# A head's rounding cast moves from the Vector engine to Pool, in a bucketed attention with a gated convolution

## The chip, the cores and the metric

The kernel runs on one core of a Trainium2 chip. The core has a matrix engine (PE, with its weight loads shown apart as PEld), a vector engine (DVE), a scalar engine (ACT), Pool (GpSimd), and SP, which here only issues DMAs. Each engine works through its own queue in order, and the engines wait for each other by semaphores. The metric is the device time of one execution in microseconds (us). "The profile" is one execution seen by the hardware profiler, "the trace" its single instructions.

## The reference

Four batches, eight heads, 768 positions, head size 64. Queries and keys are hashed into six bits, a query sees only the keys of its own bucket, and the result of the attention goes through a causal convolution of five taps, a sigmoid gate and two matrices of 512 by 512.

```python
q_bits = (np.einsum('bhsd,dk->bhsk', q, proj) > 0).astype(np.int64)
k_bits = (np.einsum('bhsd,dk->bhsk', k, proj) > 0).astype(np.int64)
mask = q_bucket[:, :, :, None] == k_bucket[:, :, None, :]
scores = scale * np.matmul(q, k.transpose(0, 1, 3, 2))
scores = np.where(mask, scores, -1000000000.0)
attn = np.exp(scores - np.max(scores, axis=-1, keepdims=True))
attn = attn / (np.sum(attn, axis=-1, keepdims=True) + 1e-09)
attn_out = np.matmul(attn, v)
# x is attn_out with the heads side by side, xp is x with 4 rows of zeros ahead
for k in range(K):
    gate_pre += conv_w[k][None, None, :] * xp[:, k:k + S, :]
gate = 1.0 / (1.0 + np.exp(-gate_pre))
val = x @ w_val
return (gate * val @ w_out).astype(np.float32)
```

## The kernel before

**Units and tiles.** A unit is one head of one batch, 32 in all. A unit has six tiles of 128 queries, so there are 192 tiles, and the main loop makes one step (k) for each. A step works on several tiles at once, each at another stage: the row maxima of tile k (`nm`, L238, DVE), a factor and a shift for each row (`gs` L244, `nb` L248, DVE), the scores of tile k+1 (`s`, L232, PE), the exponentials of tile k (`p`, L256, ACT, with the row sums by the accumulator), the row sums and reciprocals of tiles k-2 and k-1 (L262 and `ri` L266, DVE, on even steps), the normalisation of tile k-2 (L271, Pool, in place), the transposes of tile k-3 (`tp`, L280, PE), and their copies to SBUF (`pt`, L289, ACT). The product with the values (`av`, L303, PE) follows in pieces.

**Exactness by two parts.** The scores are made by matmuls in the rounded type fp32r. A head's queries and keys, which lie in one tile `r` of 128 rows (64 of queries, 64 of keys), are split into a rounded part and a remainder. `prep(i)` does it for unit i: it takes four tiles (`aq`, `ak`, `bq`, `bk`, from a pool `stk` with two of each), writes the rounded copy of `r` into `aq` (L166), the remainder `r - aq` into `bq` (L168, Pool), and six DMAs on SP then put the halves where the two score matmuls want them: `ak<-aq` and `bk<-aq` (L169, L170), `bk<-bq` (L171), `bq<-aq` (L172), and the bits of the hash, `aq<-u` and `ak<-u` (L174, L175). The last line also asks for the tile `r` of a unit five further on (L147). The first unit has its own way (`first_prep`).

**When it runs.** `prep(i+1)` is a generator. It is started in the last step of unit i-1, so a whole unit of six tiles lies between its start and the first scores that need it, and each step takes one piece of it: the cast in one step, the subtraction with the DMAs in the next. With it run other generators: the weights (`load_weights`, `split_weight`, `from_float64`: in the shape that the timed kernel is given they come as 64-bit floats and are unpacked by L90 on ACT, L92, L93, L96, L99, L100 and L108 on DVE, L110 and L112 on Pool; two tiles `w` take turns), the convolution (L332, L334 on DVE, one tap for each step), and the second half (`moe`: L365, L390 on PE, L370, L374 on DVE, `hl` L376 on Pool; `xh` L323 and `xl` L324 split its input). The weights are unpacked beside the first nine units; from then on the second half of a batch runs beside the next batch.

**What sets the order.** On PE, DVE, ACT and Pool the order of the instructions is the order of the code (`manual_schedule`). The order of SP's DMAs is left to the framework, which places them by its own estimate of when each can go. So a change in the code of one engine can reorder SP's queue.

Of the kernel before, what the change touches and what calls it, by code (L numbers as in the profile page):

```python
# [26 lines left out]
def kernel(  # L27
# [10 lines left out]
    nc = tc.nc  # L38
# [104 lines left out]
    def load_raw(i):  # L143
        if i < len(units):
            b, h = units[i]
            raws[i] = raw.tile([P, S], FP32, name="r")
            nc.sync.dma_start(out=raws[i], in_=qk[b, h])  # L147

    def load_values(i):
        b, h = units[i]  # L150
        if h % 2 == 0:
            vts[i] = vp.tile([P, KB, P], FP32, name="vt")
            nc.sync.dma_start(out=vts[i], in_=v[b, h // 2])
        else:
            vts[i] = vts[i - 1]

    def prep(i):

        if i >= len(units):
            return  # L160
        b, h = units[i]
        j = h % 4
        load_values(i)
        r = raws[i]
        aq, ak, bq, bk = stacks[i] = [stk.tile([P, S], FP32R, name=nm) for nm in ("aq", "ak", "bq", "bk")]
        nc.vector.tensor_copy(out=aq, in_=r)  # L166
        yield
        nc.gpsimd.tensor_tensor(out=bq, in0=r, in1=aq.bitcast(FP32), op=ALU.subtract)  # L168
        nc.sync.dma_start(out=ak[0:D].bitcast(FP32), in_=aq[D:P].bitcast(FP32))  # L169
        nc.sync.dma_start(out=bk[0:D].bitcast(FP32), in_=aq[D:P].bitcast(FP32))  # L170
        nc.sync.dma_start(out=bk[D:P].bitcast(FP32), in_=bq[D:P].bitcast(FP32))  # L171
        nc.sync.dma_start(out=bq[D:P].bitcast(FP32), in_=aq[0:D].bitcast(FP32))  # L172
        u = cur["u"]
        nc.sync.dma_start(out=aq[D:M].bitcast(FP32), in_=u[32 * j:32 * j + 2 * NB].bitcast(FP32))  # L174
        nc.sync.dma_start(out=ak[D:M].bitcast(FP32), in_=u[32 * j + 2 * NB:32 * j + 4 * NB].bitcast(FP32))  # L175
        load_raw(i + 5)
        if j == 3 and i + 1 < len(units):
            yield
            yield from bits(i + 1)
# [6 lines left out]
    def bits(i):  # L186

        u = stk.tile([P, S], FP32R, name="u", bufs=2)
        for hf in range(2):
            yield  # L190
            sl = slice(hf * HS, (hf + 1) * HS)
            z = side_tile()
            for jj in range(4):
                nc.tensor.matmul(out=z[32 * jj:32 * jj + 32, 0:HS], lhsT=proj_sb,
                                 rhs=raws[i + jj][:, sl], start=True, stop=True,
                                 tile_position=(0, 32 * jj))
            nc.vector.tensor_scalar(out=u[:, sl], in0=z[:, 0:HS], scalar1=rows_sb[:, 0:1], scalar2=rows_sb[:, 1:2],
                                    op0=ALU.is_ge, op1=ALU.mult)
        cur["u"] = u
# [242 lines left out]
    with tc.manual_schedule(engines=ENGINES):  # L442
# [3 lines left out]
        first_prep()  # L446
        weights = [[load_conv(), load_weights(0)], [load_weights(1)]]
        preps = [first_bits(), prep(1)]
        scores(0)
        step(weights[0])  # L450
        step(weights[1])
        turn = 0
        for k in range(N + LAG + 1):
# [15 lines left out]
            if k + 1 < N:  # L469
                if tiles[k + 1][0] != tiles[k][0]:  # L470
                    finish(preps)
                    preps = [prep(tiles[k + 1][0] + 1)]
                scores(k + 1)
# [83 lines left out]
```

## Time and profile before

| | |
|---|---|
| median of 3 runs | 639.09 us (638.87 to 639.24) |
| the profiled execution | 637.56 us |
| its span, first to last instruction | 635.6 us |
| mean granted clock of PE | 0.989 |
| cast L166, 31 times on DVE | 20.6 us |
| subtraction L168, 31 times on Pool | 58.4 us |
| normalisation L271, 192 times on Pool | 220.0 us |

A row of the timeline reads: start, duration, engine, line, operation, output and inputs, shape, how often, and in brackets the idle time of the engine ahead of it with what ended that. SPq is the queue in which SP issues its DMAs. In the table by stretch each engine's busy time stands with its number of instructions, then the granted clock of PE, the share of the DMA engines and their rate. A row of the chain of waits is a start, a length and what the end waited for in that time. A line like L166 is a line of the program printed above.

### The profile page before, as it was taken

Reading aid. Unit: us, or ns where it says so; the run is one execution under the profiler, and the core shown is the slowest. Engines: PE = TensorE matmul, PEld = TensorE weight load, DVE = VectorE, ACT = ScalarE, POOL = GpSimd, SP = SyncE. Lnnn points to the kernel's source line nnn. Section 1 sums busy time; section 2 is a strip of 40 time slices with the busy share of each in tenths; the row PEclk is TensorE's granted clock in tenths of the full one; section 3 lists DMA queues with packets and bytes.
Section 4 is the critical chain, followed back from the end, with each engine's and each line's share of the span. In section 5 each row is a group of like instructions: output and inputs, shape, how many; then the busy total and the mean of one; then the engine's idle time right before and its main releaser. Section 6 shows DMA issues by size and latency. Waiting matters only on the chain.

```text
span 635.6 us, 10630 instructions
## 1 busy us (share of the span) xinstructions
PE 590.1 (93%) x3496; PEld 424.3 (67%) x3496; DVE 465.9 (73%) x1064; ACT 421.7 (66%) x881; POOL 364.7 (57%) x326
## 2 busy tenths in 40 slices
PE   4689888878999999999999999999999999999997
PEld 2465554555567777676667877677667777776895
DVE  5789897999986766668675877578685787665532
ACT  3487776767778666667787766677778677675400
POOL 1375868577765764567653776466562677544221
PEclk9899998998999999999999999999999999999999
DMA  6533535443332334343433333343422223300111
GB/s 243 128 101 86 139 96 138 112 134 81 104 80 58 83 75 123 82 105 96 104 80 79 88 80 110 80 121 80 120 57 61 57 53 79 86 18 2 50 51 50
DMA packets 23269, 56.76 MB, mean 89 GB/s; under 512 B 4296, under 2 KB 4296, under 8 KB 23216
## 3 DMA queue, kind: packets, MB, share of 16 engines
q1 hardware_dynamic: 23072, 56.06, 32.9%
q8 instruction: 28, 0.46, 0.3%
q14 instruction: 25, 0.20, 0.1%
q10 hardware_dynamic: 144, 0.03, 0.0%
HBM read 23.12 MB, written 6.29 MB: 46 GB/s over the span
## 4 chain that ended last, share of the span: by engine, by line
PE 64%; DVE 18%; ACT 10%; issue 3%; DMA 3%; POOL 0%; DVEq 0%; ACTq 0%
PE av L303 16%; PE s L232 15%; PE tp L280 12%; PE m L390 8%; PE m L365 7%; DVE nm L238 6%; ACT p L256 4%; DVE g L334 3%; ACT pt L289 3%; ACT x L311 2%; DMA w<-in_w_out_dram 2%; DVE aq L166 1%; PE tp L365 1%; PE tp L390 1%; PE s L390 1%
## 5 line engine op out<-in xcount | busy, mean ns | idle before, releaser
L271 POOL TENSOR_SCALAR p<-p,ri 128x768 f32<-128x768 f32 x192 | 220.0, 1150 | 200.3 <-DVE nb L248 157.6
L256 ACT ACTIVATE p<-s,nb,gs 128x768 f32<-128x768 f32 x192 | 192.7, 1004 | 49.7 <-DVE nb L248 44.6
L289 ACT COPY pt<-tp 128x384 f32<-128x384 f32 x384 | 166.2, 485 | 86.0 <-PE tp L280 85.0
L238 DVE TENSOR_REDUCE nm<-s 128x1 f32<-128x768 f32 x192 | 182.4, 950 | 52.8 <-PE s L232 52.6
L280 PEld LDWEIGHTS tp<-ident,p 128*128 128x128 f32 x1152 | 130.4, 142 | 74.2 <-issue 47.3
L280 PE MATMUL tp<-ident,p 128*128 128x128 f32 x1152 | 165.4, 280 | 4.5 <-ACT pt L289 1.6
L232 PE MATMUL s<-ak,aq 76*128 76x384 f32 x384 | 118.6, 390 | 32.2 <-ACT p L256 25.4
L303 PE MATMUL av<-pt,vt 128*64 128x384 f32 x768 | 146.9, 504 | 0.0
L232 PE MATMUL s<-bk,bq 128*128 128x384 f32 x384 | 101.6, 346 | 0.0
L232 PEld LDWEIGHTS s<-ak,aq 76*128 76x128 f32 x384 | 59.4, 195 | 48.9 <-ACT p L256 39.3
L303 PEld LDWEIGHTS av<-pt,vt 128*64 128x64 f32 x768 | 47.4, 137 | 63.3 <-issue 62.7
L334 DVE SCALAR_TENSOR_TENSOR g<-x,cw_sb,g 128x768 f32<-128x768 f32 x64 | 78.4, 1225 | 0.2
L232 PEld LDWEIGHTS s<-bk,bq 128*128 128x128 f32 x384 | 71.9, 194 | 0.5 <-issue 0.5
L376 POOL TENSOR_TENSOR hl<-ht,hh 128x384 fp32r<-128x384 f32 x32 | 33.4, 1044 | 45.5 <-DVE hh L374 45.5
L168 POOL TENSOR_TENSOR bq<-r,aq 128x768 fp32r<-128x768 f32 x31 | 58.4, 1885 | 0.5 <-DVE aq L166 0.5
L311 ACT COPY x<-av 64x384 f32<-64x384 f32 x64 | 30.4, 475 | 33.5 <-PE av L303 32.9
L365 PE MATMUL m<-xh,wv 128*128 128x384 f32 x200 | 42.7, 337 | 0.0
L248 DVE TENSOR_SCALAR nb<-nm,gs 128x1 f32<-128x1 f32 x192 | 40.1, 209 | 3.5
L370 DVE TENSOR_TENSOR ht<-m,g 128x384 f32<-128x384 f32 x25 | 13.9, 555 | 35.4 <-PE m L365 32.0
L256 ACT ACTIVATION_READ_ACCUMULATOR p<-s,nb,gs 128x1 f32 x192 | 39.1, 204 | 0.0
L324 POOL TENSOR_TENSOR xl<-x,xh 128x384 fp32r<-128x384 f32 x32 | 33.5, 1066 | 9.5 <-DVE xh L323 9.5
L390 PE MATMUL m<-wo,hh 128*128 128x512 f32 x144 | 38.1, 394 | 0.0
(84 smaller groups left out, 475.6 us busy)
## 6 DMA issues: line engine op xcount, KB each, us to landing
r<-in_qk_dram SPq DMA_DIRECT2D x32, 384.0 KB
vt<-in_v_dram SPq DMA_DIRECT2D x16, 384.0 KB
out_dram<-o SPq DMA_DIRECT2D x24, 256.0 KB
ak<-aq SPq DMA_DIRECT2D x31, 192.0 KB
bk<-aq SPq DMA_DIRECT2D x31, 192.0 KB
bk<-bq SPq DMA_DIRECT2D x31, 192.0 KB
bq<-aq SPq DMA_DIRECT2D x31, 192.0 KB
w<-in_w_val_dram SPq DMA_DIRECT2D x4, 512.0 KB
```

Of the source, the lines that this page charges most:

```text
L168: nc.gpsimd.tensor_tensor(out=bq, in0=r, in1=aq.bitcast(FP32), op=ALU.subtract)
L232: nc.tensor.matmul(out=s[:, hf, 0:HS], lhsT=lq[0:n, qs], rhs=rk[0:n, hf * HS:(hf + 1) * HS], start=n == M, stop=n == P)
L238: nc.vector.tensor_reduce(out=nm, in_=s[:, :, 0:HS], axis=AX.XY, op=ALU.max, negate=True)
L256: nc.scalar.activation(out=p, in_=s[:, :, 0:HS], func=AF.Exp, bias=nb, scale=gs.pop(k), accum_out=sm[:, k % 2, 0:1])
L271: nc.gpsimd.tensor_scalar(out=p, in0=p, scalar1=rcs.pop(k), scalar2=1.0, op0=ALU.mult, op1=ALU.mult)
L280: nc.tensor.transpose(out=tp[:, n * P:(n + 1) * P], in_=p[:, kb * P:(kb + 1) * P], identity=ident)
L289: nc.scalar.copy(out=pt[:, :, qo:qo + P], in_=tp[:, 0:HS].rearrange("p (a b) -> p a b", b=P))
L303: nc.tensor.matmul(out=av[s * D:(s + 1) * D, 0:HS], lhsT=vt[:, kb, hh * D:(hh + 1) * D], rhs=pt[kb // 3][:, kb % 3, :], start=(kb == 0), s ...
L311: nc.scalar.copy(out=x[hh * D:(hh + 1) * D, o:o + HS], in_=av[s * D:(s + 1) * D, 0:HS])
L334: nc.vector.scalar_tensor_tensor(out=g, in0=x[:, k:k + S], scalar=w, in1=g, op0=ALU.mult, op1=ALU.add)
L365: nc.tensor.matmul(out=acc[:, 0:HS], lhsT=wv[wi][:, c, j * P:(j + 1) * P], rhs=xs_[(c, o)][xi], start=(m == 0), stop=(m == 11))
L390: nc.tensor.matmul(out=acc, lhsT=hs[(o, j)][hi][:, tb * P:(tb + 1) * P], rhs=wo[wi][:, j, :], start=(m == 0), stop=(m == 11))
```

## The change

One line: the rounded copy of a head's `r` into `aq` is made by Pool instead of DVE. The subtraction that follows, the DMAs, the tiles and the place in the generator stay as they were.

```diff
         aq, ak, bq, bk = stacks[i] = [stk.tile([P, S], FP32R, name=nm) for nm in ("aq", "ak", "bq", "bk")]
-        nc.vector.tensor_copy(out=aq, in_=r)
+        nc.gpsimd.tensor_copy(out=aq, in_=r)
         yield
         nc.gpsimd.tensor_tensor(out=bq, in0=r, in1=aq.bitcast(FP32), op=ALU.subtract)
```

What that moves, at three places. First Pool, in a unit whose step also has weights to split (`w_848` is a weight tile, `p` the tile that is normalised); a plus marks a row that only the changed kernel has here:

```order
 L271 TENSOR_SCALAR p<-p,ri 128x768 x4
 L110 TENSOR_TENSOR w_848<-w_848,wv_118 128x512
+L166 CAST aq<-r 128x768
 L271 TENSOR_SCALAR p<-p,ri 128x768
 L168 TENSOR_TENSOR bq<-r,aq 128x768
```

The cast stands one normalisation ahead of the subtraction, as it belongs to the step before it, and it follows the weights' subtraction directly.

Then DVE at the same place in the program (`s_1182` is the pair of row sums, `nm` the row maxima of the next tile):

```order
 L334 SCALAR_TENSOR_TENSOR g<-x,cw_sb,g 128x768
 L96 SCALAR_TENSOR_TENSOR w_950<-w_950,o 128x512
-L166 CAST aq<-r 128x768
 L238 TENSOR_REDUCE nm<-s 128x1
 L262 TENSOR_SCALAR s_1182<-sm 128x2
```

The cast is gone between the last weight operation of one step and the row maxima of the next.

Last SP's queue, the DMAs behind that unit's subtraction (`r` is the load of a unit five further on, `vt` the values, `w_1273` a weight tile):

```order
 L170 DMA bk<-aq 64x768
 L171 DMA bk<-bq 64x768
-L147 DMA r<-in_qk_dram 128x768
-L153 DMA vt<-in_v_dram 128x768
-L172 DMA bq<-aq 64x768
-L174 DMA aq<-u 12x768
+L174 DMA aq<-u 12x768
+L153 DMA vt<-in_v_dram 128x768
+L172 DMA bq<-aq 64x768
+L147 DMA r<-in_qk_dram 128x768
 L136 DMA w_1273<-in_w_out_dram 128x1024
 L175 DMA ak<-u 12x768
```

The load of `r` went from directly behind `bk<-bq` to directly ahead of the weights, and the bits `aq<-u` went to the front. The same is found at the next such load (`w_1712`), and at the one before (`w_848`) only the bits moved forward.

## The prediction

> **What bounds the kernel now.** I read the page's busy times first, then the chain of work that ended last with its shares by line, then busy time by stretch.
>
> ```profile
> span 635.6 us, 10630 instructions
> PE 590.1 (93%) x3496; PEld 424.3 (67%) x3496; DVE 465.9 (73%) x1064; ACT 421.7 (66%) x881; POOL 364.7 (57%) x326
> core 0: us, PE busy (x) PEld busy (x) DVE busy (x) ACT busy (x) POOL busy (x), PEclk, DMA share, GB/s
> 80.00:100.00 20.00, 16.79 (x94) 10.81 (x96) 19.62 (x41) 14.59 (x33) 13.47 (x12) 0.94 0.38 90
> 520.00:560.00 40.00, 40.00 (x239) 30.30 (x240) 26.91 (x65) 28.77 (x63) 22.29 (x20) 1.00 0.29 74
> by line: PE av L303 16.5%; PE s L232 15.4%; PE tp L280 11.7%; PE m L390 7.9%; PE m L365 6.6%; DVE nm L238 6.0%; ACT p L256 4.3%; DVE g L334 3.1%; issue 3.1%; ACT pt L289 2.7%; ACT x L311 2.0%; DMA w<-in_w_out_dram 1.7%; DVE aq L166 1.4%; PE
> ```
>
> PE is the bound of the whole, 590.1 of 635.6 us, but not of every stage. From 520 to 560 us it is busy all 40.00 us, and DVE with 26.91 has room. From 80 to 100 us it is DVE that is full (19.62 of 20.00) and PE waits 3.2 us. So DVE time is worth something up to about 165 us, where the weights are unpacked beside the heads, and next to nothing after it. The cast that moves stands in the chain with 1.4% of 635.6 us, that is 8.9 us: the ceiling of the gain. The group and its places in the chain (start, us):
>
> ```profile
> L166 DVE CAST aq<-r 128x768 fp32r<-128x768 f32 x31 | 20.6, 665 | 0.2
> 20.54 1.05 DVE aq L166
> 60.73 0.46 DVE aq L166
> 76.30 1.39 DVE aq L166
> 94.17 0.47 DVE aq L166
> 111.99 0.55 DVE aq L166
> 130.18 0.47 DVE aq L166
> 146.75 1.39 DVE aq L166
> 163.95 0.47 DVE aq L166
> 320.62 0.47 DVE aq L166
> ```
>
> 31 casts cost 20.6 us of DVE; a third of them is in the chain at all. The other twenty are hidden by PE; taking them away gives nothing.
>
> **What the cast costs on Pool.** No row of before shows a one-input cast on Pool. The nearest is Pool's own normalisation, also one input and the same tile size:
>
> ```profile
> 109.67 0.91 POOL L271 TENSOR_SCALAR p<-p,ri 128x768 f32<-128x768 f32 x1
> ```
>
> The other end is the two-input subtraction L168 with 1.82 us (its row stands below). I see no reason for less than 0.9. I take 0.91, the row it is nearest to, where DVE leaves it alone, and keep 1.82 for the range.
>
> [...]
>
> In the late stage the cast falls into Pool's idle time ahead of the next normalisation. The tightest place, Pool and then PE's transposes of the last tile:
>
> ```profile
> 436.29 1.67 POOL L271 TENSOR_SCALAR p<-p,ri 128x768 f32<-128x768 f32 x1 [0.48 <-ACT pt L289]
> 439.75 1.62 POOL L271 TENSOR_SCALAR p<-p,ri 128x768 f32<-128x768 f32 x1
> 442.28 0.85 PE L280 MATMUL tp<-ident,p 128*128 128x128 f32 x6 [0.16 <-ACT pt L289]
> ```
>
> Pool idles 0.48 us where the cast of 0.91 goes, so what stands behind it comes 0.43 us later; the normalisation that ends at 441.37 is used at 442.28, 0.91 us of slack. Nothing is lost; with 1.82 us it would be 1.34 late and cost PE 0.43 here.
>
> **Where the removal pays.** The place at 76.30, DVE, Pool, ACT and PE:
>
> ```profile
> 76.07 1.20 POOL L112 TENSOR_TENSOR wv<-w 128x512 fp32r<-128x512 f32 x1
> 76.30 1.39 DVE L166 CAST aq<-r 128x768 fp32r<-128x768 f32 x1
> 78.92 0.68 DVE L96 SCALAR_TENSOR_TENSOR w<-w,o 128x512 int32<-128x512 int32 x1
> 79.10 0.99 ACT L256 ACTIVATE p<-s,nb,gs 128x768 f32<-128x768 f32 x1 [0.95 <-DVE nb L248]
> 80.35 1.82 POOL L168 TENSOR_TENSOR bq<-r,aq 128x768 fp32r<-128x768 f32 x1
> 80.83 1.76 DVE L332 TENSOR_SCALAR g<-x,cw_sb 128x768 f32<-128x768 f32 x1
> ```
>
> The rows show a hold: DVE's cast started 0.23 us after Pool's L112 and ended 0.42 after it (77.69 against 77.27), and L332 ended 0.42 after L168 (82.59 against 82.17). A DVE copy, or a DVE operation with two inputs in SBUF, that starts second waits for Pool's instruction to end. The new cast is one more such instruction: 77.27 to 78.18. Without L166 the chain on DVE would reach L96 at 77.53, 1.39 earlier; it is held to 78.18. L96 then runs to about 78.75, Pool's normalisation takes 0.91 behind it, so L168 starts near 79.63 and not at 80.35, and L332 ends 0.72 earlier. **Gain 0.72**, not 1.39.
>
> At 94.17 the same hold turns against the change:
>
> ```profile
> 91.46 1.29 POOL L110 TENSOR_TENSOR w<-w,wv 128x512 f32<-128x512 f32 x1
> 92.01 1.56 DVE L334 SCALAR_TENSOR_TENSOR g<-x,cw_sb,g 128x768 f32<-128x768 f32 x1
> 93.49 0.68 DVE L96 SCALAR_TENSOR_TENSOR w<-w,o 128x512 int32<-128x512 int32 x1
> ```
>
> Pool's cast is ready when L110 ends at 92.75, waits for L334 to 93.57 and runs to 94.4; L96, held behind it, ends near 95.03. Now DVE is through with L96 and its own cast at 94.64 (94.17 and 0.47 in the chain), and the reduction nm follows: it will start 0.39 later than now. **A loss of 0.39**, and the same at 130.18.
>
> At 146.75 the wait of PE is long, so the full 1.39 comes back; PE is then in the chain on its own for some 9 us:
>
> ```profile
> 150.69 0.61 PE L232 MATMUL s<-ak,aq 76*128 76x384 f32 x2 [2.08 <-ACT p L256]
> 153.00:156.00 3.00, 3.00 (x14) 2.29 (x11) 2.96 (x8) 2.14 (x5) 2.48 (x4) 0.56 0.71 205
> 156.00:159.00 3.00, 3.00 (x20) 1.73 (x18) 2.68 (x5) 2.59 (x6) 0.77 (x1) 1.00 0.32 70
> 159.00:162.00 3.00, 2.76 (x20) 2.33 (x19) 2.35 (x9) 2.25 (x6) 2.10 (x3) 1.00 0.05 8
> ```
>
> Behind the idle 2.08 us PE's granted clock is 0.56 for 3 us: 1.3 us of work lost. With 0.7 us of idle time I expect this stretch to go; DVE, which is next with idle 0.04, 0.32 and 0.65 us in these rows, lets some **0.8** through.
>
> [...]
>
> The rest: 44.25 gives 0.23 (ACT waits no longer than that), 60.73 gives 0.46, 111.99 gives 0.55, 163.95 gives 0.47, 320.62 and its like near 466 us give 0.2 each, since the cast holds L334 for part. At 20.54 there is nothing to gain:
>
> ```profile
> 46.19 0.99 ACT L256 ACTIVATE p<-s,nb,gs 128x768 f32<-128x768 f32 x1 [0.23 <-DVE nb L248]
> 28.06 0.98 PE L232 MATMUL s<-ak,aq 76*128 76x384 f32 x2 [2.31 <-issue]
> ```
>
> PE stands 2.31 us until the second head's copies have landed. The subtraction, now behind cast and normalisation, ends some 0.4 later, and with it the last copy (bq<-aq, L172); the first half of the scores does not need that one. I charge **0.2**.
>
> **What moves on SP's queue.** In the unpacking stage the load of a later head (r) goes from ahead of the value tile to just ahead of the weight load:
>
> ```profile
> 101.99 0.48 SPq L172 DMA_DIRECT2D bq<-aq  x1
> 103.52 6.17 DMA w<-in_w_out_dram
> r<-in_qk_dram SPq DMA_DIRECT2D x32, 384.0 KB
> w<-in_w_out_dram SPq DMA_DIRECT2D x4, 512.0 KB
> 109.72 0.71 ACT L90 ACTIVATE o<-w 128x512 f32<-128x512 f32 x1 [0.82 <-DMA w<-in_w_out_dram]
> ```
>
> ACT already waits 0.82 us for this weight tile, and its 6.17 us from issue to landing are in the chain. r will now go out behind L172, just ahead of it, and travel in its time. Bound: nothing, or the whole travel of r, by the weights' own rate 6.17 x 384 / 512 = 4.6 us. I take **1.0**, nearer to nothing, since the bytes that go out up to the weights are the same as before and only their start is later. The next such load (w_1712) I leave at 0 for the same reason.
>
> **Sum.** 0.23 + 0.46 + 0.72 - 0.39 + 0.55 - 0.39 + 1.39 + 0.47 + 0.4 = 3.44; clock 0.8; minus 0.2 and 1.0: **3.0 us less**. The profiled execution took 637.56 us, 1.96 over its span; the median of the runs is 639.09, 1.5 above it, and I take the difference off the median: **636.1 us**.
>
> **Rivals.**
> - *DVE's L96 gets in ahead of Pool's cast* at 94.17 and 130.18. Then both give 0.47: 1.7 us more, **634.4**. For it: DVE's instructions follow each other without a gap. Against: Pool has been waiting since 92.75. 15%.
> - *The slow clock stays* at 153 us, or comes at another place: **636.9**. 10%.
> - *A slow cast*, 1.82 us: at 20.54, 76.30, 94.17 and 130.18 another 0.91 each, 3.6 in all: **639.7**, no change. 13%.
> - *The weights come late* (slower). At both loads that now have r directly ahead, the weights wait for all of r, 4.6 us each instead of 1.0 and 0; ACT holds its queue for each. The change without any lateness is worth 3.44 + 0.8 - 0.2 = 4.0, so it decides from 4.0 us of lateness in all: 639.1 - 4.0 + 9.2 = **644.3**, and half of it already gives 639.7. For it: L90 waits now, and the load is in the chain. Against: the bytes ahead of the weights are the same. 10%.
> - *The cast doesn't move the chain*: Pool reaches it so late that the copies to ak and bk, on SP behind it, hold the next head. It would show as PE waiting for DMAs at a head's first tile; the copies have five tiles of time, so 4%, near **639**.
>
> **How the numbers follow.** The forecast has the remaining 48%. The range takes the first rival with a full return of the weights' 1.0 at the lower end, and, at the upper, the slow cast and rather more than half of the late weights: 632.8 to 640.5. About 0.2% (1.3 us) is what a measurement can tell from no change. Faster by more than it: most of the forecast, the first rival and most of the second, 0.63; within it, 0.22; slower, 0.15.
>
> **What would show it.** Right: a Pool cast near 0.9 us alone and up to 1.6 behind a DVE operation; DVE busy by some 20 us less, PE idle by some 3 us less and only up to 165 us; L96 at 94 us ended later than L334 by a Pool cast; L90 waiting about 1.5 us for the weights. Wrong: a cast over 1.3 us alone, transposes that wait for Pool after 200 us, or a span that changes after 200 us by more than 1 us.

## The result, and the profile after

| | before | changed |
|---|---|---|
| median | 638.98 us (637.55 to 639.24, 4 runs) | 632.86 us (632.47 to 634.94, 4 runs) |
| the profiled execution | 637.56 us | 634.94 us |
| its span | 635.6 us | 633.2 us |

The ratio is 0.991, with a 95% interval of 0.9883 to 0.9937. The forecast was 636.1 us, 3.0 less than before; measured here are 6.1 less, and 4.6 less in a second series further below. The profiled execution of the changed kernel is the longest of its four, so its trace shows less of the gain than the median does. That has to be explained too.

From the page of the changed kernel: the busy times, the shares of the chain by engine, and two groups of instructions (the number behind the bar is the busy time, the next one the mean in ns).

```profile
PE 591.4 (93%) x3496; PEld 426.2 (67%) x3496; DVE 451.3 (71%) x1033; ACT 421.1 (67%) x881; POOL 386.0 (61%) x357
PE 69%; ACT 14%; DVE 12%; issue 2%; DMA 2%; POOL 0%; SPq 0%; ACTq 0%; POOLq 0%; DVEq 0%
L166 POOL CAST aq<-r 128x768 fp32r<-128x768 f32 x31 | 27.8, 897 | 0.0
L96 DVE SCALAR_TENSOR_TENSOR w<-w,o 128x512 int32<-128x512 int32 x8 | 8.0, 1002 | 0.0
```

DVE lost the 20.6 us of its casts, yet its busy time fell by 14.6 only. Of the 6.0 us between, about 3.5 went into other DVE instructions that now take longer (L96 1.9 us, L262 2.4, L92 and L93 0.7 each, and some take a little less); the other 2.5 us are overlap, since the records of the casts reached into those beside them and busy time counts such a stretch once. The row of L96 in the kernel before shows it at 760 ns:

```profile
L96 DVE SCALAR_TENSOR_TENSOR w<-w,o 128x512 int32<-128x512 int32 x8 | 6.1, 760 | 0.0
```

Where the gain is, the table by stretch tells: first the stage with weights and then the one without, of before and then of the changed kernel.

```profile
0.00:165.00 165.00, 133.45 (x768) 87.17 (x769) 142.22 (x312) 111.22 (x237) 102.77 (x93) 0.96 0.44 122
200.00:600.00 400.00, 392.37 (x2370) 286.98 (x2370) 283.22 (x663) 282.10 (x588) 232.33 (x207) 1.00 0.31 80
```

```profile
0.00:165.00 165.00, 136.25 (x777) 90.16 (x778) 138.99 (x308) 113.00 (x241) 114.02 (x105) 0.95 0.44 122
200.00:600.00 400.00, 393.14 (x2372) 288.12 (x2373) 276.17 (x646) 279.43 (x586) 240.49 (x225) 1.00 0.31 79
```

In the first 165 us PE is busy 2.8 us longer and gets through 777 matmul instructions where it was 768. From 200 to 600 us PE is busy 393.1 of 400 us and was 392.4: nothing to win there, with the cast gone from DVE or not.

Two places of the changed kernel in rows of the timeline. At 92 us, the hold that the prediction charged:

```profile
91.61 1.55 DVE L334 SCALAR_TENSOR_TENSOR g<-x,cw_sb,g 128x768 f32<-128x768 f32 x1
92.29 1.55 POOL L166 CAST aq<-r 128x768 fp32r<-128x768 f32 x1
93.08 1.31 DVE L96 SCALAR_TENSOR_TENSOR w<-w,o 128x512 int32<-128x512 int32 x1
96.92 1.01 PE L232 MATMUL s<-ak,aq 76*128 76x384 f32 x2 [2.33 <-ACT p L256]
```

Pool's cast is issued at 92.29 and stands behind L334, which ends at 93.16; it ends at 93.84, 0.68 us later. L96, issued at 93.08, ends only 0.55 us behind that: 1.31 us, where it took 0.68 at this place before. At 148 us, where the prediction expected most:

```profile
147.86 0.82 POOL L166 CAST aq<-r 128x768 fp32r<-128x768 f32 x1
148.25 0.98 DVE L96 SCALAR_TENSOR_TENSOR w<-w,o 128x512 int32<-128x512 int32 x1
149.56 0.62 PE L232 MATMUL s<-ak,aq 76*128 76x384 f32 x2 [0.41 <-ACT p L256]
153.00:156.00 3.00, 2.44 (x15) 1.64 (x15) 2.97 (x8) 2.59 (x6) 2.40 (x3) 1.00 0.89 232
```

PE waits 0.41 us where it waited 2.08, and the granted clock behind it is 1.00 where it was 0.56.

### The profile page after: what moved, and what is told of

Its sections match the earlier page's. It is cut to its first block, busy times and chain, and to the rows that moved or that the text cites. A ratio compares the mean times of both kernels' runs of the same rounds, so it can differ in the third digit from the quotient of the medians.

```text
span 633.2 us, 10639 instructions
## 1 busy us (share of the span) xinstructions
PE 591.4 (93%) x3496; PEld 426.2 (67%) x3496; DVE 451.3 (71%) x1033; ACT 421.1 (67%) x881; POOL 386.0 (61%) x357
## 4 chain that ended last, share of the span: by engine, by line
PE 69%; ACT 14%; DVE 12%; issue 2%; DMA 2%; POOL 0%; SPq 0%; ACTq 0%; POOLq 0%; DVEq 0%
PE av L303 19%; PE s L232 17%; PE tp L280 12%; PE m L390 8%; PE m L365 7%; ACT p L256 6%; ACT pt L289 4%; DVE nm L238 3%; ACT x L311 3%; PE tp L365 1%; PE tp L390 1%; PE s L390 1%; DVE u L197 1%; PE tp L194 1%; DVE g L334 1%
## 5 line engine op out<-in xcount | busy, mean ns | idle before, releaser
L271 POOL TENSOR_SCALAR p<-p,ri 128x768 f32<-128x768 f32 x192 | 215.9, 1129 | 173.8 <-DVE nb L248 149.6
L238 DVE TENSOR_REDUCE nm<-s 128x1 f32<-128x768 f32 x192 | 182.5, 951 | 64.3 <-PE s L232 64.2
L303 PE MATMUL av<-pt,vt 128*64 128x384 f32 x768 | 147.6, 506 | 0.0
L303 PEld LDWEIGHTS av<-pt,vt 128*64 128x64 f32 x768 | 47.6, 137 | 63.7 <-issue 63.1
L334 DVE SCALAR_TENSOR_TENSOR g<-x,cw_sb,g 128x768 f32<-128x768 f32 x64 | 77.9, 1217 | 0.2
```

Of the source, the lines that this page charges most:

```text
L238: nc.vector.tensor_reduce(out=nm, in_=s[:, :, 0:HS], axis=AX.XY, op=ALU.max, negate=True)
L271: nc.gpsimd.tensor_scalar(out=p, in0=p, scalar1=rcs.pop(k), scalar2=1.0, op0=ALU.mult, op1=ALU.mult)
L303: nc.tensor.matmul(out=av[s * D:(s + 1) * D, 0:HS], lhsT=vt[:, kb, hh * D:(hh + 1) * D], rhs=pt[kb // 3][:, kb % 3, :], start=(kb == 0), s ...
L334: nc.vector.scalar_tensor_tensor(out=g, in0=x[:, k:k + S], scalar=w, in1=g, op0=ALU.mult, op1=ALU.add)
```

## The experiments

All kernels but the first, which is the changed kernel again, differ from it in the engine of this one cast, for some units (and one makes a second cast); `i` is the unit. "Pool 1 to 10" below is the kernel with the cast on Pool for units 1 to 10 (the stage with weights) and on DVE behind them.

| cast on | median us (range, runs) | before, same series | ratio, 95% interval |
|---|---|---|---|
| Pool, all (the change again) | 633.59 (632.70 to 635.84, 6) | 638.17 | 0.9928, 0.9912 to 0.9944 |
| Pool 1 to 10, DVE behind | 632.98 (632.43 to 633.83, 4) | 638.17 | 0.9917, 0.9903 to 0.9931 |
| DVE 1 to 10, Pool behind | 638.15 (637.16 to 639.29, 11) | 638.17 | 0.9999, 0.9990 to 1.0009 |
| ACT 1 to 10, Pool behind | 631.20 (630.26 to 632.04, 4) | 638.17 | 0.9888, 0.9873 to 0.9902 |
| Pool 5 and 9 only | 636.10 (635.37 to 637.51, 8) | 638.07 | 0.9974, 0.9962 to 0.9985 |
| Pool 1 to 10 without 5 and 9 | 636.45 (634.95 to 638.75, 12) | 638.07 | 0.9973, 0.9958 to 0.9987 |
| DVE, and a second one on Pool | 642.69 (642.01 to 644.39, 6) | 638.07 | 1.0078, 1.0064 to 1.0093 |
| Pool 2 to 10 | 633.84 (633.17 to 634.96, 6) | 638.07 | 0.9934, 0.9921 to 0.9947 |
| Pool 1 to 10, but 6 and 8 on ACT | 632.06 (631.60 to 632.13, 4) | 638.38 | 0.9897, 0.9880 to 0.9913 |
| Pool 1 to 10, but 6 and 8 on DVE | 633.21 (632.54 to 633.51, 4) | 638.38 | 0.9916, 0.9901 to 0.9931 |
| ACT 2 to 10, DVE else | 631.23 (630.75 to 632.34, 4) | 638.38 | 0.9889, 0.9873 to 0.9905 |
| ACT, all | 632.06 (630.80 to 632.81, 6) | 637.77 | 0.9904, 0.9885 to 0.9923 |

The kernels do not all have the same order of DMAs on SP. The weight loads that are issued near 103 and 139 us and unpacked near 109 and 144 us have `r` directly ahead of them in the changed kernel, the change again, Pool 1 to 10, Pool 2 to 10 and Pool 1 to 10 without 5 and 9; in the others, those with ACT and those with 6 and 8 on ACT or DVE among them, the DMA directly ahead is the one of before. No kernel changes that order alone; what can be said of it stands with the prediction's terms below.

To read a trace place by place, I compare the start of the row maxima (L238) of each of the 192 tiles with the same tile in the trace before, and take by how much this lead or lag changes from the last tile of one head to the second of the next. That is what a place costs (+) or returns (-), in us, whatever came ahead of it. The first column is the time of the place in the trace before.

```
place        Pool again  Pool 1-10  Pool 2-10  dup    ACT 1-10  6, 8 on ACT  6, 8 on DVE
44.7         -0.48       -0.47      -0.47     +0.63   -0.47     -0.47        -0.48
61.1         -0.48       -0.49      -0.49     +0.65   -0.44     -0.47        -0.45
77.6         -1.06       -1.07      -0.39     +0.72   -1.21     -1.05        -1.01
94.6         +0.16       +0.16      +0.15     +0.62   -0.48     -0.48        -0.01
130.6        +0.16       +0.16      +0.17     +0.64   -0.47     -0.46         0.00
148.1        -1.22       -1.05      -1.03     -0.68   -1.31     -0.99        -1.82
```

("dup" is the kernel with a second cast on Pool. Where a slow stretch that starts between 131 and 139 us stands ahead of the place at 148.1, as in dup and in the kernel with 6 and 8 on DVE, part of its loss seems to be made good there.)

### The change once more, and its two halves

**The change again**, to see what of 3.0 against 6.1 us is chance:

> The changed kernel once more, with several runs of both kernels on one chip. The two profiled executions differ by 2.6 us, the medians by 6.1. Theory A (the gain is the casts on DVE's chain, some 2.5 to 4 us, and the rest is in which stretches of the first 160 us PE's clock is granted at half): the runs of each kernel spread over about 2 to 3 us, the difference of the medians lies between 3 and 6 us, and an execution with no half-clock stretch has the shorter span. Rival B (the profile hides a gain that is there in every run): the difference stays at 6 us with both spreads under 1 us.

Measured: 633.59 us, 4.6 below the before of its series; with the first four, ten executions of the changed kernel lie between 632.47 and 635.84. The gain is real in each of them, and how large it is varies by 3 us.

**Pool in the stage with weights only:**

```diff
-        nc.gpsimd.tensor_copy(out=aq, in_=r)
+        (nc.gpsimd if i <= 10 else nc.vector).tensor_copy(out=aq, in_=r)
```

> The cast runs on Pool for units 1 to 10 only, from unit 11 on DVE as before. Theory A: all of the gain lies in the stage in which the weights are unpacked; the time is that of the changed kernel within 0.6 us (0.2 us each may be lost at two places near 319 and 465 us). Rival C (Pool and DVE trade time in the late stage too, and PE gains there): at least a third of the gain, 2 us, is lost.

**Pool behind it only:**

```diff
-        nc.gpsimd.tensor_copy(out=aq, in_=r)
+        (nc.gpsimd if i > 10 else nc.vector).tensor_copy(out=aq, in_=r)
```

> The cast runs on DVE for units 1 to 10 as before, from unit 11 on Pool. Theory A: the time of the kernel before, at most 0.6 us less. Rival C: 2 us or more below the kernel before.

Measured: 632.98 and 638.15 us. The first half is the whole change (5.2 us, not distinguishable from 4.6); the second half is worth nothing to within 0.1%. At the two places late in the run for which the prediction wrote 0.2 us each, the row maxima come 0.12 us earlier in the trace, and two tiles later that is gone.

**ACT in place of Pool in the stage with weights:**

```diff
-        nc.gpsimd.tensor_copy(out=aq, in_=r)
+        if i <= 10:
+            nc.scalar.copy(out=aq, in_=r)
+        else:
+            nc.gpsimd.tensor_copy(out=aq, in_=r)
```

> The cast runs on ACT for units 1 to 10 and on Pool from unit 11. It is DVE's relief without Pool's new instruction in the early stage. Theory A with the hold (a Pool cast holds DVE's L96 at 94 and 130 us by some 0.6 us, at 76 and 147 by 0.3): about 1.5 to 2 us under the changed kernel, less what ACT's own cast of some 0.8 us delays of the exponentials. Rival D (the hold costs nothing, since DVE's chain waits for PE anyway): not below the changed kernel, and above it by the ACT time, up to 0.8 us for each of ten units.

Measured: 631.20 us, better than both kernels. The same place as above in its trace (the added lines shift the numbers by three: L235 is the score matmul):

```profile
91.44 0.83 ACT L167 CAST aq<-r 128x768 fp32r<-128x768 f32 x1
91.75 0.68 DVE L96 SCALAR_TENSOR_TENSOR w<-w,o 128x512 int32<-128x512 int32 x1
94.96 0.62 PE L235 MATMUL s<-ak,aq 76*128 76x384 f32 x2 [1.33 <-ACT p L259]
```

ACT needs 0.83 us for the cast, Pool alone 0.82, but L96 takes 0.68 us beside it and not 1.31, and PE waits 1.33 and not 2.33 us.

### Two places alone, and the others

```diff
-        nc.gpsimd.tensor_copy(out=aq, in_=r)
+        (nc.gpsimd if i in (5, 9) else nc.vector).tensor_copy(out=aq, in_=r)
```

> The cast is on Pool for units 5 and 9 alone (the places at 76.30 and 146.75 us of the trace before, where the vector engine's cast took 1.39 us behind Pool's), and on the vector engine for the other 29; SP's order of DMAs is that of before. Theory A (these two places and the slow-clock stretch behind the second carry most of the gain): about 1.0 us from the first, 1.1 from the second and 1.05 from the stretch at 153 us, 3.1 us below before, 635.1 (634.3 to 636.0); PE waits about 0.4 us at the first scores of unit 9 and not 2.1. Rival E (each moved cast returns about the same): two tenths of the 5.2 us of the kernel with units 1 to 10 on Pool, about 1 us below before.

```diff
-        nc.gpsimd.tensor_copy(out=aq, in_=r)
+        (nc.gpsimd if i in (1, 2, 3, 4, 6, 7, 8, 10) else nc.vector).tensor_copy(out=aq, in_=r)
```

> The complement: the cast is on Pool for units 1, 2, 3, 4, 6, 7, 8 and 10, on the vector engine for units 5, 9 and those behind 10. Theory A: the returns at 44, 60, 112 and 164 us (0.48, 0.48, 0.57, 0.47) less the first head switch (0.74) and the two held weight operations (0.15 each), so about 0.5 to 1 us below before, 637.5 (636.8 to 638.2), with PE's wait of 2.1 us and the slow stretch near 153 us still there; up to 1.1 us less in executions where the stretch near 98 us is missing. Rival E: eight tenths of 5.2 us, about 4.2 us below before.

Measured: 2.0 us and 1.6 us below before. Neither theory met both numbers: A wanted 3.1 and 0.5 to 1, E about 1 and 4.2. The two do not even add up to the 5.2 us of Pool 1 to 10. The traces say why. With units 5 and 9 alone the place at 77.6 us returned 0.38 and not 1.0; what decides that is shown below. And two things come and go between executions of one kernel: the slow clock (the kernel with the eight units ran from 634.95 to 638.75, and its trace, at 638.37, has slow stretches at 98, 132 and 153 us and a mean granted clock of 0.984), and the wait for weights near 109 us.

### A second cast on Pool: the price without the return

```diff
-        nc.gpsimd.tensor_copy(out=aq, in_=r)
+        nc.vector.tensor_copy(out=aq, in_=r); i <= 10 and nc.gpsimd.tensor_copy(out=bq, in_=r)
```

> The vector engine keeps its cast, and for units 1 to 10 Pool makes the same rounded copy once more, into the tile bq, which the subtraction overwrites a step later: the price of the cast on Pool without the return of the one on the vector engine. Theory A: a Pool cast of 0.82 us that holds L96 near 94 and 130 us, 0.6 us each, the first head switch 0.7, and up to 0.8 us each at the places near 76 and 147 us where the vector engine's cast stands behind it: 1.3 to 3.5 us over before, about 640.2. Rival D (the hold costs nothing, since the vector engine is late there anyway): within 0.6 us of before.

Measured: 4.6 us over before, above the expected 1.3 to 3.5. Rival D falls. The table by places shows the price at each: 0.63, 0.65, 0.72, 0.62 and 0.64 us. In its trace near 95 us:

```profile
95.47 1.56 POOL L166 CAST bq<-r 128x768 fp32r<-128x768 f32 x1
96.27 1.31 DVE L96 SCALAR_TENSOR_TENSOR w<-w,o 128x512 int32<-128x512 int32 x1
97.50 0.55 DVE L166 CAST aq<-r 128x768 fp32r<-128x768 f32 x1
```

Behind the first head switch, I had expected the price at the places near 76, 94, 130 and 147 us only. It is paid at 44.7 and 61.1 us as well, since DVE's own cast stands behind it there (near 61 us that cast takes 1.20 us, and 0.53 in the trace of before). With the table this closes: at 94.6 and 130.6 us the second cast costs 0.62 to 0.64, taking the cast off DVE without a hold (the ACT column) returns 0.46 to 0.48, and the difference, 0.16, is what the change costs there. At 44.7 and 61.1 us Pool returns the full 0.48: the next DVE instruction there is the row maxima, and in the changed kernel's trace they take 0.94 us beside Pool's cast (45.05 and 61.11 us), as they did in the trace of before (44.72 and 61.13).

### The first head switch, and the weights at 74 us

```diff
-        nc.gpsimd.tensor_copy(out=aq, in_=r)
+        (nc.gpsimd if 2 <= i <= 10 else nc.vector).tensor_copy(out=aq, in_=r)
```

> The cast is on Pool for units 2 to 10, on the vector engine for unit 1 and those behind 10. Theory A: the first head switch is as before (PE waits about 2.3 us at 28 us, not 3.4), which returns 0.7 us: 632.3 (631.6 to 633.0) where units 1 to 10 on Pool gave 632.98. Rival F (the early lateness is made good later, since another engine is late at 44 us): the same as units 1 to 10 on Pool within 0.3 us.

Measured: 633.84 us, 0.9 slower than Pool 1 to 10, so neither theory held: the first head switch has its 0.5 us back, and more is lost later. By the two traces that is 0.7 us at the place near 77.6 us, and 0.9 at a slow stretch near 98 us that this trace has and that of Pool 1 to 10 has not; the second is chance, as shown further below. The place at 77.6 us has two forms. First the changed kernel's profiled execution, then the change again (rows of ACT, DVE and Pool):

```profile
74.91 0.69 ACT L90 ACTIVATE o<-w 128x512 f32<-128x512 f32 x1 [0.60 <-DMA w<-in_w_val_dram]
74.93 0.89 POOL L271 TENSOR_SCALAR p<-p,ri 128x768 f32<-128x768 f32 x1
75.63 0.48 DVE L92 TENSOR_SCALAR o<-o 128x512 f32<-128x512 f32 x1 [0.74 <-ACT o L90]
75.80 1.20 POOL L112 TENSOR_TENSOR wv<-w 128x512 fp32r<-128x512 f32 x1
76.14 1.14 DVE L93 TENSOR_SCALAR o<-o 128x512 int32<-128x512 int32 x1
77.21 0.94 DVE L238 TENSOR_REDUCE nm<-s 128x1 f32<-128x768 f32 x1
79.84 0.62 PE L232 MATMUL s<-ak,aq 76*128 76x384 f32 x2 [0.84 <-ACT p L256]
```

```profile
74.30 0.68 ACT L90 ACTIVATE o<-w 128x512 f32<-128x512 f32 x1
74.97 1.15 POOL L271 TENSOR_SCALAR p<-p,ri 128x768 f32<-128x768 f32 x1
75.00 0.43 DVE L92 TENSOR_SCALAR o<-o 128x512 f32<-128x512 f32 x1
75.47 0.93 DVE L93 TENSOR_SCALAR o<-o 128x512 int32<-128x512 int32 x1
76.09 1.20 POOL L112 TENSOR_TENSOR wv<-w 128x512 fp32r<-128x512 f32 x1
76.32 0.94 DVE L238 TENSOR_REDUCE nm<-s 128x1 f32<-128x768 f32 x1
79.24 0.62 PE L232 MATMUL s<-ak,aq 76*128 76x384 f32 x2 [0.24 <-ACT p L256]
```

In the second form the weights are there, L92 takes its 0.43 us, and Pool's normalisation is the one that waits (1.15 us against 0.89); the row maxima start at 76.32. In the first, the weights land 0.6 us late, L93 meets Pool's L112 and ends 0.28 us behind it (77.28 against 77.00; in the second form 0.28 us behind the normalisation, 76.40 against 76.12), and the row maxima start 0.89 later. The place returned 1.01 to 1.21 us in the five traces where L90 did not wait there (the change again, Pool 1 to 10, ACT 1 to 10, and 6 and 8 on ACT or on DVE), and 0.38 to 0.40 in the five where L90, or L92 behind it, waited 0.17 us or more (the changed kernel's profile, Pool 2 to 10, Pool 5 and 9, ACT 2 to 10, ACT all). Theory H was tested with ACT 2 to 10:

```diff
-        nc.gpsimd.tensor_copy(out=aq, in_=r)
+        if 2 <= i <= 10:
+            nc.scalar.copy(out=aq, in_=r)
+        else:
+            nc.vector.tensor_copy(out=aq, in_=r)
```

> The cast is on the scalar engine for units 2 to 10, on the vector engine for unit 1 and those behind 10. The kernel with units 2 to 10 on Pool was 0.9 us slower than that with 1 to 10, though PE waited 0.7 us less at the first head switch; its trace shows L90 waiting 0.41 us for the weights at 74 us. Theory H (a lead won ahead of 74 us is lost there, as the weights land at their own time, and L92 and L93 then stand behind Pool's normalisation): no faster than units 1 to 10 on the scalar engine, 631.2 to 632.0, with a wait of L90 at 73 to 74 us. Rival F': 0.4 us faster, 630.8, as the first head switch is as before.

Measured: 631.23 us, the same as ACT 1 to 10, with L90 waiting 0.18 us at 74.09 and a return of 0.40. That is theory H's number, but the two traces do not bear out its reason: at the last tile ahead of the place both are 0.4 us ahead of before, so there was no further lead to lose, and both issue this load at 69.60 us. ACT 1 to 10 can start L90 at 73.77, the other only at 74.09. So the load itself took longer in one execution, and theory H is not shown. The order on SP does not settle it either: late and timely weights occur with both orders. Why they land up to 0.6 us later in one execution than in another is open.

### The two held places

```diff
-        nc.gpsimd.tensor_copy(out=aq, in_=r)
+        if i in (6, 8):
+            nc.scalar.copy(out=aq, in_=r)
+        else:
+            (nc.gpsimd if i <= 10 else nc.vector).tensor_copy(out=aq, in_=r)
```

> The cast is on the scalar engine for units 6 and 8 (the places at 94.09 and 130.10 us of the trace before), on Pool for the other units up to 10, on the vector engine behind 10. Theory A' (what the scalar engine's version has over Pool's is the hold of the weight operation L96 at these two places, with the wait of PE behind it, which is long enough there to bring the slow clock): L96 takes 0.68 us and not 1.31, PE's wait at the first scores of both units falls from 2.4 to about 1.3 us, no slow stretch begins there; 0.6 us at each place and in part of the executions 1.1 us for a slow stretch, so about 631.3 (630.6 to 632.1) where units 1 to 10 on Pool gave 632.98 and units 1 to 10 on the scalar engine 631.2. Rival G (its lead is from the first head switch and the other places): 632.5 or more.

```diff
-        nc.gpsimd.tensor_copy(out=aq, in_=r)
+        (nc.gpsimd if i <= 10 and i not in (6, 8) else nc.vector).tensor_copy(out=aq, in_=r)
```

> The cast is on Pool for units 1 to 5, 7, 9 and 10, on the vector engine for units 6 and 8 and those behind 10. Theory A': the two held places lose 0.15 us each on Pool, so 0.3 us below the 632.98 of units 1 to 10 on Pool, 632.7 (632.0 to 633.6), with L96 at 0.68 us, and with PE's waits there still at 2.1 to 2.2 us and so the slow clock behind them in part of the executions. Rival G: the same time within 0.2 us, as these two places do not matter.

Measured: 632.06 and 633.21 us. With ACT the two places return 0.48 and 0.46 where Pool costs 0.16 each, 1.26 us in all, and no slow stretch stands behind them (the eight matmuls of L306 take 1.51 us at both); the median is 0.9 below Pool 1 to 10, so theory A' has about half of the lead of ACT 1 to 10 (1.8 us), and other places the rest. (These two kernels also have the DMA order of before at the loads named above, so the cast is not quite the only thing that differs from Pool 1 to 10.) With DVE the places stand at 0, as expected, 0.16 each less than with Pool, but the time does not show it (633.21 against 632.98): its trace has a slow stretch near 97 us that the other does not have (L303 0.37 us for each matmul against 0.19).

### ACT for all heads

```diff
-        nc.gpsimd.tensor_copy(out=aq, in_=r)
+        nc.scalar.copy(out=aq, in_=r)
```

> The cast is on the scalar engine for all 31 units. With units 1 to 10 there and the rest on Pool it took 631.2 us. Theory J (behind unit 10 the engine of the cast is hidden under PE, whichever it is): 631.2 (630.4 to 632.1), with no step behind 200 us that is later than in the kernel with units 1 to 10 there. Rival K (the scalar engine's exponentials and copies are what PE waits for behind 200 us, so a cast of 0.84 us ahead of them comes through): 0.2 to 0.5 us at each of 21 heads, 635.5 to 642.

Measured: 632.06 us, within J's interval at its upper end. The trace has one loss behind 190 us, 0.73 us between 200 and 215; after it the last tiles of the heads keep their distance to within 0.2 us up to 450 us. K's loss at every head is not there.

## Why the prediction was right, and where its sizes were not

The forecast held in its mechanism: the gain is in the stage with weights, it is the chain over DVE, Pool holds (L96 takes 1.31 us behind its cast and not 0.68) and is held (the cast takes 1.55 us behind L334 and not 0.82), and the slow clock at 153 us goes (1.00 where it was 0.56). The size it had too small: 632.86 us is only 0.06 above the lower end of its range, and that the time stayed inside owes something to chance, as the terms and the clock show. Term by term, with Pool 1 to 10 and the change again as the measure:

- **Pool's cast, 0.91 us predicted.** It takes 0.82 alone and 1.55 behind a DVE operation (predicted: to 1.6). The rival of a slow cast falls.
- **44 us: 0.23 predicted, 0.48 measured,** of which 0.13 is lost two tiles later. **61 us: 0.46 and 0.48.** **164 us: 0.47 and 0.38,** where a loss of 0.08 stands ahead of a return of 0.46.
- **76 us: 0.72 predicted; 1.06 where the weights are there, 0.39 where they are late.** In the timely form, the one that the prediction worked from, it charged too much: in the change again, where all stands 0.07 us later ahead of the place, Pool's cast ends at 78.06 (predicted 78.18) and the subtraction starts 1.28 us behind it and not 1.45, since the normalisation between them starts as the cast ends and does not wait for L96. The late form it left out.
- **94 and 130 us: a loss of 0.39 each predicted, 0.16 measured.** The mechanism is exactly the one described (L96 at 1.31 us behind Pool's cast); the price was too high, as Pool's cast is done 0.68 us behind the end of L334 and not 0.9: L96 ended 1.23 us behind L334 (94.39 against 93.16), not 1.46 as predicted (95.03 against 93.57). The rival that L96 gets in ahead falls: it did so in no trace with Pool's cast there.
- **147 us: 1.39 predicted, 1.05 to 1.22 measured** (1.57 in the changed kernel's profile). The prediction took the full return; L96 is held here too, 0.97 or 0.98 us and not 0.68. With ACT, where L96 takes 0.68, the place returns 1.31. **The slow stretch behind it: 0.8 predicted, 1.03 measured.** It is gone in each trace with unit 9's cast off DVE, and there in three of the four with it there.
- **320 and 466 us: 0.2 each predicted, nothing measured.** Those rows stand in the chain, but what they give back (0.12 us of the row maxima) is gone two tiles later.
- **First head switch: 0.2 predicted, 0.39 to 0.73 measured.** How much of it is the cast's is not shown. The kernels with DVE's cast on this unit (DVE 1 to 10, Pool 5 and 9, Pool 2 to 10, ACT 2 to 10) lose 0.20 to 0.64 against the trace of before as well. The prediction said that the first half of the scores does not need the last copy (`bq<-aq`). The second half does, and there PE waits 0.02 to 0.36 us in the six traces with Pool's cast in place of DVE's and not at all in the five with DVE's alone; the larger wait is the one ahead of the first half, 1.5 to 3.5 us in all traces.
- **112 us with the late weights w_1273: a return of 0.55 and a loss of 1.0 predicted, 0.45 lost in all.** Measured: 0.44 lost in the change again, but 0.27 returned in Pool 1 to 10 and 0.40 in the changed kernel's profile, where L90 does not wait there at all. The runs do not show that the new order on SP makes the weights late: L90 waits here for 0, 0.45, 1.06, 1.07 and 1.31 us in the five traces with `r` directly ahead, and for 0 to 1.30 us in the nine without (before 0.82, DVE 1 to 10 1.30). So the 1.0 us that was charged for the order has nothing behind it, the rival of late weights falls, and the wait changes between executions of one kernel (0 and 1.07). It comes at the load near 74 us too, which the prediction left out.

The sum of the terms as predicted is 3.0, as measured in the trace of Pool 1 to 10 it is 4.5 (its span is 631.1 against 635.6). The largest single item of the difference was not in the prediction at all: the trace of before has a slow stretch near 98 us, and that of Pool 1 to 10 has none (1.16 us). The prediction says nothing of it. PE's wait ahead of it stays (2.16 us before, 2.34 with Pool 1 to 10); whether the stretch comes is chance, as shown next. It also explains why the profiled execution, 634.94 us, shows less than the median: it has that stretch, doubled in length, one near 134 us, and the late form at 76 us (0.67 us). Over the executions it is not chance alone: the mean granted clock has a median of 0.989 in the 17 executions of before in the second series and of 0.9945 in the ten of the changed kernel. By these, half speed lasts about 7 us less in all, an estimate; one stretch of 3.4 us of it would be the one behind 147 us; where the rest falls is not shown.

## What to carry to other kernels

Before moving work from DVE to Pool, look at what stands *behind* it on DVE. Here the row maxima ran on beside Pool's cast (0.94 us with and without it, and 0.48 us came back), while L96, issued during that cast, took 1.31 us and not 0.68, and 0.16 us was lost where ACT's cast returned 0.46 to 0.48. Where ACT has idle time at the same place, it can take the work: beside its cast L96 took 0.68 us. And in a stage bound by several engines, terms of half a microsecond did not add up across these kernels (2.0 and 1.6 us for the two parts of a change worth 5.2): measure each place in the trace, and take more than one execution.

## What the runs showed of the hardware that was not expected

**The clock.** In the trace of before, up to 620 us, the granted clock is halved from 25.96, 97.64 and 152.26 us on, for 6.83, 3.41 and 3.41 us; in that of the changed kernel from 28.33, 96.60 and 134.14 us on, for 6.83, 6.83 and 3.41 us. From one start to the next it is 21 and 16 times 3.413 us in the first trace, 20 and 11 times in the second. Both traces are divided here into windows of that length, counted from these starts, from 21 to 620 us. In seven of them PE is idle for 1.78 us or more (1.78, 1.85, 2.10 and 2.16 in the first; 2.01, 2.38 and 3.20 in the second), and the window behind each of these is slow. In all others PE is idle for 1.41 us or less, and of the windows behind them only two are slow, both the second half of a stretch of 6.83 us in the changed kernel. Between the two figures other traces show both: with the second cast on Pool 1.68 us idle (115.08 to 118.49) and a clock of 0.50 behind it, with Pool 2 to 10 1.65 us (127.90 to 131.31) and 1.00. In the table by stretch, each window and the one behind it; PE's busy time is the first number behind the comma, the granted clock the third from the right. Before:

```profile
94.19:97.60 3.41, 1.25 (x9) 1.01 (x8) 3.38 (x9) 1.58 (x5) 1.62 (x2) 1.00 0.53 114
97.60:101.02 3.42, 3.42 (x12) 1.09 (x10) 3.35 (x7) 1.35 (x3) 3.25 (x2) 0.51 0.20 43
```

The change again, with two waits of the same length (2.33 and 2.38 us):

```profile
92.30:95.71 3.41, 1.70 (x14) 1.42 (x11) 3.38 (x9) 1.38 (x3) 1.55 (x2) 1.00 0.39 86
95.71:99.13 3.42, 2.81 (x16) 1.61 (x17) 3.35 (x5) 2.31 (x6) 3.42 (x3) 1.00 0.15 31
129.84:133.25 3.41, 1.49 (x8) 0.99 (x10) 3.32 (x9) 1.83 (x4) 2.70 (x2) 1.00 0.53 114
133.25:136.66 3.41, 3.41 (x14) 2.00 (x11) 3.04 (x8) 2.68 (x6) 2.85 (x3) 0.50 0.43 90
```

Of the first wait (93.99 to 96.32) 1.71 us lie in the one window and the rest in the next, and the clock stays at 1.00; of the second (129.38 to 131.76) 1.92 us of idle time lie in one window, and the clock behind it is 0.50. From the first scores behind the wait to those of the next tile it is 2.97 us at the first (96.32 to 99.29) and 4.34 at the second (131.76 to 136.10). So of two waits of the same length in one trace one cost 1.4 us more than the other, and with two or three such waits in a run that is of the size of the 3 us between executions of one kernel. That it is decided by where a window ends is my reading of these rows; no run varies that alone. With ACT at 94 and 130 us PE waits 1.33 or 1.34 us, and in the traces of ACT 1 to 10, ACT 2 to 10 and 6 and 8 on ACT the eight matmuls of L306 behind it take 1.51 us each time, where those of L303 take 2.83 in the slow stretch of before (98.36 us).

**DVE and Pool.** At each place where a DVE copy or two-input operation stood behind the second cast on Pool, 0.62 to 0.72 us was lost; where the row maxima stood behind Pool's cast (44.7 and 61.1 us), 0.48 us was returned in full; and L96 took 0.68 us beside ACT's cast. Of two that wait, Pool's cast, issued at 92.29 while L334 ran, came ahead of L96, issued at 93.08. The prediction speaks of copies and of operations with two inputs. The trace of before has both: DVE's cast takes 1.39 us at 76.30 and 146.75, behind Pool's L112, and 0.55 at 44.25; L96 takes 1.31 us at 59.43, behind Pool's L110, and 0.68 at 93.49. But it is not they alone: L93 has one input, and the rows near 76 us above show it 0.28 us behind the end of Pool's instruction in both forms.
